# Row transposes as row pairs, and one layer norm on GpSimd, in a two-chain recurrent attention kernel

## The chip, the cores and the metric

The kernel runs on one core of a Trainium2 chip. Five engines work side by side in it: TensorE (PE; its weight loads are listed as PEld), VectorE (DVE), ScalarE (ACT), GpSimd (POOL) and SyncE (SP), which only issues transfers here. The metric is the device time of one execution in microseconds (us), the median of the runs. Lower is better.

## The reference, cut to what matters

Four layers in a row, each on the layer norm of its input and with a residual: attention with a recurrent memory (A), a gated feed-forward (B), A again and B again, with the same weights both times.

```
x = x + A(layernorm(x), mem0, Wq, Wk, Wv, Wo, seg_len=32)
x = x + B(layernorm(x), W_gate, W_up, W_down)
x = x + A(layernorm(x), mem0, Wq, Wk, Wv, Wo, seg_len=32)
x = x + B(layernorm(x), W_gate, W_up, W_down)

A: mem = mem0                                  # 8 rows of 448
   for each of 64 segments of 32 rows:
       h = concat(mem, rows)                   # 40 x 448
       p = softmax(mask(h Wq (h Wk)^T / 16))   # 16 heads of 256; rows are causal, memory is seen by all
       o = (p h Wv) Wo
       mem, out = o[:8], o[8:]
B: (relu(x W_gate) * (x W_up)) W_down          # 448 -> 1792 -> 448
```

x is 2048 x 448 in bf16. A segment needs the memory that the segment before it left, so attention is a chain of 64 links.

## The kernel before, in words

**Preparation.** Wq and Wk of each head are multiplied into one 448 x 448 matrix (tiles A_sb, A3, A3z), Wv and Wo into another (B_sb). Per head, scores are then rows x A x rows^T, and the output is p x rows x B. This ends some 72 us into the execution.

**Steps.** The rest is 69 steps (L591, `step(g, ff)`; the last, g = 68, only projects). The two attention layers run as two chains: step g does segment g of the first (chain 0) and segment g - 4 of the second (chain 1), in one set of matmuls; the chain is a block of columns (64 apart) of the transposed rows hT. From g = 4 to 63 both chains run, at the ends only one. Scores and weights for new memory rows (Sm, PM) and for segment rows (Sx, PX) are kept apart; hf is the half of the heads.

**Order.** TensorE's instructions keep the order in which the program writes them (`in_order`, L73). The tile framework sets the semaphores and picks the PSUM bank of each tile: seven banks serve all tiles of the tag "ps", the eighth the tag "ox". The order on VectorE and ScalarE follows the program but for small exchanges between neighbours.

Within a step of both chains TensorE does, in this order:

1. Queries: banks of PSUM named `prj`, six query tiles each. `open_banks` (L500) issues the part of the contraction over the last 64 of the 448 dimensions. It is done in *row pairs*: two matmuls of 64 rows each, one on partitions 0 to 63 and one on 64 to 127, in two banks. `close_bank` (L513) adds three full-height matmuls (128 rows) for each tile, 36 in all for two banks, 12 for the smaller banks z0 and z1, and has the bank copied to TQ (VectorE or ScalarE, 128x480) or TZ (64x320 on VectorE, then 64x320 on ScalarE). Order: open b0, b2; close b0, b2; open b1, b3, z0, z1; close z0, b1, b3; `hk_make`; close z1; open c0, c2, c1, c3; scores Sm(0); close c0, c2, c1, c3. b and z0 are heads' half 0, c and z1 half 1; z0's and z1's `prj` rows show as A3z and A_sb.
2. `hk_make` (L604): four full 128x128 transposes of hT into kps, copied to hk (rows in token order) by VectorE (128x512, L609) and, for the last 64 dimensions twice over, by ScalarE (L610).
3. PM is transposed (`flipped`: TensorE pps, VectorE copy PT), Sx(0) is made, and `weigh_m` multiplies hk by PT (ya, yb). In odd steps the feed's transposes tps follow. Then Sm(1) and Sx(1).
4. `project_out` (tile ox, B_sb as weights), the second half's weights, `project_tail`, `finish` (L726), which writes the new memory columns of hT (VectorE) and the attention output OT (ScalarE).

**The feed.** Odd steps from 3 on carry a feed-forward block (`Feed`, L400) among these: rows 0 to 63 of its tiles belong to the second B layer, 64 to 127 to the first. `residual` (L411) transposes OT back to rows (four full transposes, otp), adds them to xa (VectorE, L415, 128x448) and has `row_stats` (L156) take mean and variance (VectorE) and 1 / sqrt (GpSimd, L163 and L164). It stands between the closing of b2 and the opening of b1. `norm` (L418) calls `normed` (L167): two VectorE instructions, 448 and 64 columns, that write xn. It stands behind the closing of c0. `xposed` (L421) transposes xn (tps) into xT for the gate and up matmuls (`gate_up`, row pairs again: gate on one half of the rows, up on the other). `norm2` (L454) is the norm of the rows that go to the second attention chain; it too calls `normed`. A last feed runs by itself behind all steps.

**Row pairs elsewhere.** `flipped_rows` (L573) already transposes PM and PX in row pairs (ppr): for each 64-row half a transpose with a bank of its own, between matmuls of `gate_up`.

Of the kernel before, what the change touches and what calls it, by code (L numbers as in the profile page):

```python
# [8 lines left out]
BF = mybir.dt.bfloat16  # L9
F32 = mybir.dt.float32  # L10
I32 = mybir.dt.int32
AF = mybir.ActivationFunctionType
ALU = mybir.AluOpType
AX = mybir.AxisListType

DM = 448
# [15 lines left out]
HI = 128  # L32
HW = 5 * HI
W = 2 * L
# [6 lines left out]
ROWS = (slice(0, 64), slice(64, 128))  # L41
# [12 lines left out]
def build_kernel(ctx, tc, A_x, A_mem0, A_Wq, A_Wk, A_Wv, A_Wo, B_W_gate, B_W_up, B_W_down, out,  # L54
                 ntiles=16, nseg=64):
    nc = tc.nc
    P = nc.NUM_PARTITIONS
# [10 lines left out]
    psum = ctx.enter_context(tc.tile_pool(name="psum", bufs=7, space=bass.MemoryType.PSUM))  # L68
# [4 lines left out]
    def in_order(r):  # L73
        if last_pe[0] is not None:
            tc.add_manual_dep(r.ins, last_pe[0],
                              mybir.DependencyInfo(mybir.DependencyClass.NoSync,
                                                   mybir.DependencyReason.DATA),
                              reason="order of issue")
        last_pe[0] = r.ins.name

    def mm(*a, **k):
        in_order(nc.tensor.matmul(*a, **k))  # L82

    def tr(*a):
        in_order(nc.tensor.transpose(*a))  # L85

    def evac(eng, dst, src):
        if eng is nc.scalar:
            nc.scalar.copy(dst, src)  # L89
        else:  # L90
            eng.tensor_copy(dst, src)  # L91
# [8 lines left out]
    ident = glob.tile([P, P], BF, name="ident")  # L100
# [19 lines left out]
    for b in range(4):  # L120
        o = 0 if b % 2 == 0 else MEM
# [17 lines left out]
    for i in range(2):  # L139
        t = glob.tile([P, BLK, HW], BF, name=f"hT{i}")  # L140
# [10 lines left out]
    for hf in range(2):  # L151
        t = glob.tile([P, 5, 6, 64], BF, name=f"TQ{hf}")
        tc.keep_in_program_order(nc.gpsimd.memset(t[:], 0.0))
        TQ.append(t)

    def row_stats(t, pin=False):  # L156

        stats = p_ln.tile([P, nc.vector.BN_STATS_DIM], F32, tag="ln_stats")
        (tc.keep_in_program_order if pin else lambda i: i)(nc.vector.bn_stats(stats[:], t[:]))
        mv = p_ln.tile([P, 2], F32, tag="ln_mv")  # L160
        nc.vector.bn_aggr(mv[:], stats[:])
        rstd = p_ln.tile([P, 1], F32, tag="ln_rstd")
        nc.gpsimd.tensor_scalar(out=rstd[:], in0=mv[:, 1:2], scalar1=EPS, scalar2=None, op0=ALU.add)  # L163
        nc.gpsimd.tensor_tensor(out=rstd[:], in0=rstd[:], in1=half[:], op=ALU.pow)  # L164
        return t, mv, rstd

    def normed(stat):  # L167

        t, mv, rstd = stat
        xn = p_ln.tile([P, 512], BF, tag="ln_xn", bufs=3)  # L170
        for a, b, o in ((0, DM, 0), (384, DM, DM)):
            tc.keep_in_program_order(
                nc.vector.tensor_scalar(out=xn[:, o:o + b - a], in0=t[:, a:b], scalar1=mv[:, 0:1],  # L173
                                        scalar2=rstd[:], op0=ALU.subtract, op1=ALU.mult))
        return xn

# [201 lines left out]
    for hf in range(2):  # L378
        for name, shape, where in (("Y", [P, NT, W], YY[hf]), ("Z", [P, NT, W], YY[hf]), ("TZ", [P, 5, 128], TZ),
                                   ("PX", [P, 4, 64], PX), ("PM", [P, 2, 64], PM)):  # L380
            t = main.tile(shape, BF, name=f"{name}{hf}")
# [6 lines left out]
    OT = main.tile([P, 4, 128], BF, name="OT")  # L388
# [5 lines left out]
    for i in range(2):  # L394
        t = main.tile([P, 6, 128], BF, name=f"hk{i}")
# [4 lines left out]
    class Feed:  # L400
# [8 lines left out]
            self.nx = xp[i % 2]  # L409

        def residual(self):  # L411
            tp = psum.tile([P, 4, 128], BF, tag="ps", name="otp")
            for kd in range(4):
                tr(tp[:, kd, :], OT[:, kd, :], ident[:])
            nc.vector.tensor_tensor(self.x[:], tp[:].rearrange("p k d -> p (k d)")[:, 0:DM], self.x[:], op=ALU.add)  # L415
            self.st = row_stats(self.x)

        def norm(self):  # L418
            self.xn = normed(self.st)

        def xposed(self):  # L421
            tps = transpose_tokens(self.xn)
# [50 lines left out]
    def moving(hb, j, idx, chains, rows=slice(0, P)):  # L473

        if len(chains) == 2:
            return hb[rows, j, idx * HI:(idx + 1) * HI].rearrange("p (c k) -> p c k", k=64)[:, :, 0:L]
        c = chains[0]
        return hb[rows, j, idx * HI + 64 * c:idx * HI + 64 * c + L]
# [14 lines left out]
    def last_rows(hf, t):  # L493

        if t >= 24:
            return hf, A3z[ROWS[hf], t - 24, :]
        kd, eo, p4 = t // 8, t // 4 % 2, t % 4
        return eo, A3[ROWS[eo], hf, 4 * kd + p4, :]

    def open_banks(chains, hb, j, *which):  # L500

        n = L * len(chains)
        banks = [Bank(hf, i) for hf, i in which]
        for a, b in zip(banks[::2], banks[1::2]):
            for k in range(len(a.tiles)):
                for bk in (a, b):
                    t = bk.tiles[k]
                    r, w = last_rows(bk.hf, t)
                    mm(bk.out(t, n), w, moving(hb, j, 3, chains, ROWS[r]), start=(k == 0), stop=False,
                       skip_group_check=True)  # L510
        return banks

    def close_bank(bk, chains, hb, j, eng):  # L513

        n = L * len(chains)
        hf, N = bk.hf, len(bk.tiles)
        for t in bk.tiles:
            for kd in range(3):
                mm(bk.out(t, n), A_sb[:, kd, hf, t, :], moving(hb, j, kd, chains), start=False, stop=(kd == 2),
                   skip_group_check=True)  # L520
        ps = bk.ps
        if bk.i < 4:
            at = 2 * (bk.i // 2) + bk.i % 2
            parts = [(eng, slice(0, P), TQ[hf][:].rearrange("p g (k b) w -> p g k (b w)", b=2)[:, :, :, 32 * at:32 * at + 32], 3)]
        else:
            parts = [(nc.vector, slice(0, 64), TZ[hf][0:64, :, 0:64].unsqueeze(2), 1),
                     (nc.scalar, slice(64, 128), TZ[hf][0:64, :, 64:128].unsqueeze(2), 1)]
        for eng, rows, T, K in parts:
            T = T.rearrange("p g k (t q) -> p k t g q", q=16)
            if len(chains) == 2:  # L530
                evac(eng, T, ps[rows, 0:N * n].rearrange("p (k t g q) -> p k t g q", k=K, t=N // K, q=16))
                continue
            c = chains[0]
            src = ps[rows, 0:N * n].rearrange("p (k t w) -> p k t w", k=K, t=N // K)
            x, m = (0, SEG) if c == 0 else (MEM, 0)
            evac(eng, T[:, :, :, 2, MEM * c:MEM * c + MEM], src[:, :, :, m:m + MEM])
            evac(eng, T[:, :, :, 3 * c:3 * c + 2, :],
                 src[:, :, :, x:x + SEG].rearrange("p k t (g q) -> p k t g q", q=16))
# [47 lines left out]
    def active(g):  # L586
        return [c for c in (0, 1) if 0 <= g - c * LAG < nseg]
# [3 lines left out]
    def step(g, ff):  # L591
        chains = active(g)
        xs = active(g - 1)
        ms = [c for c in chains if g - c * LAG + 1 < nseg]
        gb, j = divmod(g, BLK)
        hb = hTb[gb % 2]
        cols = [(0, 32) if c == 0 else (48, 80) for c in xs] + [(32, 40) if c == 0 else (40, 48) for c in ms]
        lo, hi = min(a for a, _ in cols), max(b for _, b in cols)
        ox = psum.tile([P, 3, W], F32, tag="ox", bufs=1, name="ox")

        def ys(hf, later=0):
            return YY[hf][(g + later) % 2]

        def hk_make():  # L604
            kps = psum.tile([P, 4, 128], BF, tag="ps", name="kps")
            for i in range(4):
                tr(kps[:, i, :], hb[:, j, i * HI:(i + 1) * HI], ident[:])
            hk = HK[g % 2]
            nc.vector.tensor_copy(hk[:, 0:4, :], kps[:])  # L609
            nc.scalar.copy(hk[:].rearrange("p k n -> p (k n)")[:, 512:768].rearrange("p (a b) -> p a b", b=64)[:, 0::3, :],  # L610
                           kps[:, 3, :].rearrange("p (a b) -> p a b", b=64))
            return hk

        def scores_m(hf):
# [80 lines left out]

        def project_out(hf, t0, t1):

            for t in range(t0, t1):
                for mc in range(3):
                    mm(ox[:, mc, lo:hi], B_sb[:, hf, t, mc * 128:(mc + 1) * 128],  # L700
                       ys(hf)[:, t, lo:hi], start=(hf == 0 and t == 0 and mc == 0),
                       stop=(hf == 1 and t == NT - 1 and mc == 2), skip_group_check=True)
# [53 lines left out]
        close_bank(b2, chains, hb, j, nc.scalar)  # L756
        if ff is not None:
            ff.residual()
        b1, b3, z0, z1 = open_banks(chains, hb, j, (0, 1), (0, 3), (0, 4), (1, 4))
        close_bank(z0, chains, hb, j, None)  # L760
        load_some()
        close_bank(b1, chains, hb, j, nc.vector)
        close_bank(b3, chains, hb, j, nc.scalar)
        hk = hk_make()
        close_bank(z1, chains, hb, j, None)
        c0, c2, c1, c3 = open_banks(chains, hb, j, (1, 0), (1, 2), (1, 1), (1, 3))
        scores_m(0)
        close_bank(c0, chains, hb, j, nc.scalar)
        if ff is not None:
            ff.norm()  # L770
        close_bank(c2, chains, hb, j, nc.scalar)
        close_bank(c1, chains, hb, j, nc.vector)
        close_bank(c3, chains, hb, j, nc.scalar)
# [63 lines left out]
    for g in range(nsteps + 1):  # L837
        if g == LAG - 1:
            set_mem(LAG, mem0T[:].unsqueeze(2), (1,))
        i = (g - 3) // 2  # L840
        step(g, Feed(i) if g % 2 and 0 <= i < nblk + LAG // BLK - 1 else None)

    ff = Feed(nblk + LAG // BLK - 1)
# [65 lines left out]
```

## Time and profile before

| what | value |
|---|---|
| median of 3 runs | 1597.05 us (1596.65 to 1598.61) |
| the profiled execution | 1598.77 us |
| its span, first to last instruction | 1597.0 us |
| mean granted TensorE clock | 0.991 |
| an even and an odd step together, at 687 us | 44.95 us |

The profile describes one execution, which took 1598.77 us in all. A row of the timeline has the start (us from the span's start), the time to the end of the last instruction merged into the row, engine, line, operation, the tile written and the tiles read, partitions x elements, and the count; a bracket at its end says how long the engine idled before it and whom it waited for. A row of groups has the count, then the busy time in us and the mean of one in ns, then the idle time before them. Starts on TensorE are measured, ends are modelled, so the distance between two starts says what an instruction cost there.

### The profile page before, as it was taken

Reading aid. Unit: us, or ns where it says so; the run is one execution under the profiler, and the core shown is the slowest. Engines: PE = TensorE matmul, PEld = TensorE weight load, DVE = VectorE, ACT = ScalarE, POOL = GpSimd, SP = SyncE. Lnnn points to the kernel's source line nnn. Section 1 sums busy time; section 2 is a strip of 40 time slices with the busy share of each in tenths; the row PEclk is TensorE's granted clock in tenths of the full one; section 3 lists DMA queues with packets and bytes.
Section 4 is the critical chain, followed back from the end, with each engine's and each line's share of the span. In section 5 each row is a group of like instructions: output and inputs, shape, how many; then the busy total and the mean of one; then the engine's idle time right before and its main releaser. Section 6 shows DMA issues by size and latency. Waiting matters only on the chain.

```text
span 1597.0 us, 97098 instructions
## 1 busy us (share of the span) xinstructions
PE 1563.3 (98%) x44708; PEld 1433.4 (90%) x44708; DVE 1139.9 (71%) x3857; ACT 762.1 (48%) x2239; POOL 93.3 (6%) x242
## 2 busy tenths in 40 slices
PE   8989999999999999999999999999999999999997
PEld 6578899999999999999999999999999999999886
DVE  6756677777777777777777777777777777777773
ACT  6634444544444444544444445544444445544442
POOL 3110000000000000000000000000000000000000
PEclk9979999999999999999999999999999999999999
DMA  9530000000000000000000000000000000000000
GB/s 288 135 85 8 9 9 5 9 9 10 10 10 10 10 9 5 9 9 10 10 10 10 10 10 4 10 9 10 10 10 9 10 10 4 10 8 7 7 7 6
DMA packets 29464, 33.06 MB, mean 21 GB/s; under 512 B 3320, under 2 KB 28160, under 8 KB 29056
## 3 DMA queue, kind: packets, MB, share of 16 engines
q1 hardware_dynamic: 28992, 26.85, 6.3%
q8 instruction: 349, 5.72, 1.5%
q14 instruction: 59, 0.48, 0.1%
q0 software_dynamic: 64, 0.01, 0.0%
HBM read 23.18 MB, written 1.84 MB: 16 GB/s over the span
## 4 chain that ended last, share of the span: by engine, by line
PE 89%; DVE 7%; ACT 1%; issue 1%; DMA 1%; POOL 1%; SPq 0%; ACTq 0%; POOLq 0%; DVEq 0%
PE prj L82 25%; PE ox L82 25%; PE ups L82 10%; PE dps L82 6%; PE o L82 5%; PE y L82 4%; PE Sx L82 2%; PE Sm L82 2%; PE bps L82 1%; DVE TQ L91 1%; DVE xn L173 1%; PE aps L82 1%; PE tps L85 1%; PE pps L85 1%; PE kps L85 1%
## 5 line engine op out<-in xcount | busy, mean ns | idle before, releaser
L82 PEld LDWEIGHTS <-B_sb 128*128 128x128 bf16 (+1 forms) x15456 | 495.0, 103 | 29.2 <-issue 21.3
L82 PE MATMUL prj<-hT,A_sb 128*128 128x80 bf16 (+1 forms) x11424 | 441.6, 200 | 0.0
L82 PEld LDWEIGHTS <-A_sb 128*128 128x128 bf16 x11424 | 412.1, 100 | 8.3
L82 PE MATMUL ox<-Y,B_sb 128*128 128x80 bf16 (+4 forms) x5880 | 222.9, 198 | 1.8 <-DVE Y L643 1.8
L82 PE MATMUL ox<-Z,B_sb 128*128 128x80 bf16 (+2 forms) x5712 | 217.6, 199 | 1.3 <-DVE Z L643 1.3
L89 ACT CAST TQ<-prj 128x480 bf16<-128x480 f32 (+1 forms) x380 | 178.5, 497 | 83.6 <-PE prj L82 59.3
L82 PE MATMUL ups<-xT,Wgu_sb 64*128 64x128 bf16 (+1 forms) x3332 | 191.5, 214 | 2.2 <-issue 1.0
L82 PE MATMUL gps<-xT,Wgu_sb 64*128 64x128 bf16 (+1 forms) x3332 | 191.5, 214 | 0.3 <-ACT xT L425 0.3
L82 PEld LDWEIGHTS <-Wgu_sb 64*128 64x128 bf16 x6664 | 179.7, 95 | 5.5 <-issue 3.3
L91 DVE CAST TQ<-prj 128x480 bf16<-128x480 f32 (+1 forms) x228 | 129.2, 573 | 13.5 <-PE prj L82 11.3
L439 DVE SCALAR_TENSOR_TENSOR hh<-gps,ut 128x256 bf16<-128x256 f32 (+1 forms) x238 | 95.3, 407 | 48.9 <-ACT ut L438 36.4
L438 ACT CAST ut<-ups 128x256 bf16<-128x256 f32 (+1 forms) x238 | 85.4, 359 | 84.3 <-PE gps L82 66.1
L91 DVE CAST Y<-y 64x128 bf16<-64x128 f32 (+2 forms) x256 | 102.0, 419 | 13.3 <-ACT Y L89 4.3
L89 ACT CAST Y<-y 64x128 bf16<-64x128 f32 (+2 forms) x256 | 89.3, 379 | 45.6 <-DVE Y L91 42.0
L91 DVE CAST Z<-y 64x128 bf16<-64x128 f32 (+2 forms) x256 | 99.1, 418 | 12.4 <-ACT Z L89 5.5
L570 DVE COPY PT<-pps 128x128 bf16<-128x128 bf16 (+1 forms) x206 | 49.5, 254 | 79.7 <-PE pps L85 78.2
L89 ACT COPY hT<-tps 128x256 bf16<-128x256 bf16 x32 | 11.9, 372 | 197.4 <-DVE hT L91 197.4
L552 ACT ACTIVATE se<-se 128x80 f32<-128x80 f32 (+1 forms) x270 | 71.4, 298 | 67.4 <-DVE se L551 66.6
L89 ACT CAST TZ<-prj 64x320 bf16<-64x320 f32 (+2 forms) x152 | 56.2, 380 | 98.9 <-DVE TZ L91 94.3
L89 ACT CAST Z<-y 64x128 bf16<-64x128 f32 (+2 forms) x256 | 89.2, 378 | 23.8 <-DVE Z L91 17.4
L82 PEld LDWEIGHTS <-hk 40*128 40x128 bf16 (+1 forms) x1989 | 80.0, 94 | 18.6 <-issue 8.7
L558 DVE TENSOR_REDUCE ssum<-se 128x2 f32<-128x80 f32 (+1 forms) x270 | 70.8, 274 | 36.0 <-ACT se L552 33.7
(128 smaller groups left out, 2240.0 us busy)
## 6 DMA issues: line engine op xcount, KB each, us to landing
wo<-in_A_Wo_dram SPq DMA_DIRECT2D x8, 448.0 KB, 8.6
nat<-in_A_Wq_dram SPq DMA_DIRECT2D x8, 384.0 KB, 5.9
nat<-in_A_Wk_dram SPq DMA_DIRECT2D x8, 384.0 KB, 5.9
nat<-in_A_Wv_dram SPq DMA_DIRECT2D x8, 384.0 KB, 7.4
xa<-in_A_x_dram SPq DMA_DIRECT2D x32, 56.0 KB, 2.8
xa<-xp SPq DMA_DIRECT2D x32, 56.0 KB, 1.9
out_dram<-xa SPq DMA_DIRECT2D x32, 56.0 KB, 2.7
xp<-in_A_x_dram SPq DMA_DIRECT2D x30, 56.0 KB, 2.1
```

The lines of the kernel that those rows point to most:

```text
L82: in_order(nc.tensor.matmul(*a, **k))
L85: in_order(nc.tensor.transpose(*a))
L89: nc.scalar.copy(dst, src)
L91: eng.tensor_copy(dst, src)
L173: nc.vector.tensor_scalar(out=xn[:, o:o + b - a], in0=t[:, a:b], scalar1=mv[:, 0:1], scalar2=rstd[:], op0=ALU.subtract, op1=ALU.mult))
L438: nc.scalar.copy(ut[:, :, n], ups[:, :, n])
L439: nc.vector.scalar_tensor_tensor(out=hh[:, 2 * u:2 * u + 2, n], in0=gps[:, :, n], scalar=0.0, in1=ut[:, :, n], op0=ALU.max, op1=ALU.mult)
L552: nc.scalar.activation(se[:], se[:], AF.Exp, scale=SCALE)
L558: nc.vector.tensor_reduce(ssum[:], se[:], axis=AX.X, op=ALU.add)
L570: nc.vector.tensor_copy(PT[:], pps[:].rearrange("p b q -> p (b q)"))
```

## The change

There are three parts.

- A helper `flipped_dims` makes the same transposes in row pairs: eight of 64 rows to 64 columns, alternating between the halves of the partitions, each half into a bank of its own, the first into the "ox" bank, the second into a "ps" bank. `residual` and `hk_make` use it. The residual add becomes two instructions, 64-column pieces of 0, 128, 256, 384 and of 64, 192, 320. The copy of hk is split: columns of the first row half on VectorE, of the second on ScalarE; ScalarE's copy of the last dimensions reads the second bank. ox itself is now allocated by the first `project_out` of a step.
- `hk_make` moves behind the closing of z1, directly ahead of the opening of c0, c2, c1 and c3. The copies that belong to z1 move ahead of hk's with it.
- Attention's norm in the feed, `ff.norm`, moves from behind c0 to directly behind the residual, and its two instructions go to GpSimd. `norm2` and the norm of the last feed stay on VectorE.

```diff
+    def flipped_dims(name, src):
+        two = [psum.tile([P, 4, 64], BF, name=name, **where) for where in (dict(tag="ox", bufs=1), dict(tag="ps"))]
+        for kd in range(4):
+            for r in range(2):
+                tr(two[r][:, kd, :], src(r, kd), ident[ROWS[r], ROWS[r]])
+        return two
...
-    def normed(stat):
+    def normed(stat, eng=None):
...
-                nc.vector.tensor_scalar(out=xn[:, o:o + b - a], in0=t[:, a:b], scalar1=mv[:, 0:1],
+                (eng or nc.vector).tensor_scalar(out=xn[:, o:o + b - a], in0=t[:, a:b], scalar1=mv[:, 0:1],
...
         def residual(self):
-            tp = psum.tile([P, 4, 128], BF, tag="ps", name="otp")
-            for kd in range(4):
-                tr(tp[:, kd, :], OT[:, kd, :], ident[:])
-            nc.vector.tensor_tensor(self.x[:], tp[:].rearrange("p k d -> p (k d)")[:, 0:DM], self.x[:], op=ALU.add)
+            tp = flipped_dims("otp", lambda r, kd: OT[ROWS[r], kd, :])
+            xd = self.x[:].rearrange("p (c d) -> p c d", d=64)
+            for r in range(2):
+                nc.vector.tensor_tensor(xd[:, r::2, :], tp[r][:, 0:4 - r, :], xd[:, r::2, :], op=ALU.add)
...
         def hk_make():
-            kps = psum.tile([P, 4, 128], BF, tag="ps", name="kps")
-            for i in range(4):
-                tr(kps[:, i, :], hb[:, j, i * HI:(i + 1) * HI], ident[:])
+            kps = flipped_dims("kps", lambda r, kd: hb[ROWS[r], j, kd * HI:kd * HI + HI])
             hk = HK[g % 2]
-            nc.vector.tensor_copy(hk[:, 0:4, :], kps[:])
+            for r, eng in enumerate((nc.vector, nc.scalar)):
+                evac(eng, hk[:, 0:4, 64 * r:64 * r + 64], kps[r][:])
             nc.scalar.copy(hk[:].rearrange("p k n -> p (k n)")[:, 512:768].rearrange("p (a b) -> p a b", b=64)[:, 0::3, :],
-                           kps[:, 3, :].rearrange("p (a b) -> p a b", b=64))
+                           kps[1][:, 3, :].unsqueeze(1).to_broadcast([P, 2, 64]))
...
         if ff is not None:
             ff.residual()
+            ff.norm(nc.gpsimd)
         b1, b3, z0, z1 = open_banks(chains, hb, j, (0, 1), (0, 3), (0, 4), (1, 4))
...
         close_bank(b3, chains, hb, j, nc.scalar)
+        close_bank(z1, chains, hb, j, None)
         hk = hk_make()
-        close_bank(z1, chains, hb, j, None)
         c0, c2, c1, c3 = open_banks(chains, hb, j, (1, 0), (1, 2), (1, 1), (1, 3))
         scores_m(0)
         close_bank(c0, chains, hb, j, nc.scalar)
-        if ff is not None:
-            ff.norm()
         close_bank(c2, chains, hb, j, nc.scalar)
```

More of the change, by code (lines that the diff above doesn't have):

```diff
@@ L411, in residual, with norm @@
         def residual(self):
-            tp = psum.tile([P, 4, 128], BF, tag="ps", name="otp")
-            for kd in range(4):
-                tr(tp[:, kd, :], OT[:, kd, :], ident[:])
-            nc.vector.tensor_tensor(self.x[:], tp[:].rearrange("p k d -> p (k d)")[:, 0:DM], self.x[:], op=ALU.add)
+            tp = flipped_dims("otp", lambda r, kd: OT[ROWS[r], kd, :])
+            xd = self.x[:].rearrange("p (c d) -> p c d", d=64)
+            for r in range(2):
+                nc.vector.tensor_tensor(xd[:, r::2, :], tp[r][:, 0:4 - r, :], xd[:, r::2, :], op=ALU.add)
             self.st = row_stats(self.x)
-        def norm(self):
-            self.xn = normed(self.st)
+        def norm(self, eng=None):
+            self.xn = normed(self.st, eng)
         def xposed(self):
@@ L598, in step @@
         lo, hi = min(a for a, _ in cols), max(b for _, b in cols)
-        ox = psum.tile([P, 3, W], F32, tag="ox", bufs=1, name="ox")
+        ox = None
         def ys(hf, later=0):
@@ L696, in project_out @@
         def project_out(hf, t0, t1):
+            nonlocal ox
+            if ox is None:
+                ox = psum.tile([P, 3, W], F32, tag="ox", bufs=1, name="ox")
             for t in range(t0, t1):
```

## The prediction

> **What bounds the kernel now.** I read the page first (shares of the engines, then the chain that ended last), then one steady period of two steps in the view by windows.
>
> ```profile
> PE 1563.3 (98%) x44708; PEld 1433.4 (90%) x44708; DVE 1139.9 (71%) x3857; ACT 762.1 (48%) x2239; POOL 93.3 (6%) x242
> ...
> PE 89%; DVE 7%; ACT 1%; issue 1%; DMA 1%; POOL 1%; SPq 0%; ACTq 0%; POOLq 0%; DVEq 0%
> ```
> ```profile
> 687.27:732.22 44.95, 44.85 (x1287) 41.84 (x1283) 32.94 (x112) 21.77 (x64) 2.10 (x6) 1.00 0.04 9
> ```
>
> TensorE is busy 44.85 us of the 44.95 us that an even and an odd step take together; the columns behind it are weight loads, VectorE 32.94, ScalarE 21.77, GpSimd 2.10, then the granted clock, 1.00. So the time is TensorE's issue order. But a matmul's row lasts some 0.2 us while the next one starts 0.03 us later, so a short stall does not show as idle time. I therefore read the starts in the timeline and look for steps that are too long.
>
> TensorE's timeline of an odd step, around the two groups of transposes that are changed (start, length of the merged run, count at the end):
>
> ```profile
> 706.94 0.39 PE L85 MATMUL otp<-ident,OT 128*128 128x128 bf16 x4
> 707.26 0.39 PE L82 MATMUL prj<-hT,A 64*128 64x80 bf16 x12
> ...
> 707.72 1.90 PE L82 MATMUL prj<-hT,A_sb 128*128 128x80 bf16 x48
> 709.45 0.39 PE L85 MATMUL kps<-ident,hT 128*128 128x128 bf16 x4
> 709.68 0.59 PE L82 MATMUL prj<-hT,A_sb 128*128 128x80 bf16 x12
> 710.20 0.60 PE L82 MATMUL prj<-hT,A 64*128 64x80 bf16 x24
> 710.74 0.28 PE L82 MATMUL Sm<-hT,TQ 128*128 128x80 bf16 x3
> ...
> 710.89 2.75 PE L82 MATMUL prj<-hT,A_sb 128*128 128x80 bf16 x72
> 713.47 0.22 PE L85 MATMUL pps<-ident,PM 128*128 128x128 bf16 x1
> ```
>
> Three prices come out of the starts. A full-height matmul of 80 columns: 48 from 707.72 to 709.45, 1.73 us, 0.036 each. A full transpose: 709.45 to 709.68, 0.23 us for four, 0.057 each. The turn from full-height work to work in row pairs: 709.68 to 710.20 is 0.52 for twelve matmuls that need 0.43, so the turn costs 0.09 more. The otp group, 706.94 to 707.26, is 0.32: four transposes and one such turn. Neither group is late; they cost what they issue.
>
> The third place is further down the step. TensorE, odd step, then the same place in the even step:
>
> ```profile
> 713.91 0.18 PE L82 MATMUL Sx<-hT,TZ 128*128 128x40 bf16 x1
> 714.18 0.27 PE L82 MATMUL ya<-PT,hk 128*128 128x128 bf16 x2
> ...
> 714.40 0.39 PE L85 MATMUL tps<-ident,xn 128*128 128x128 bf16 x4
> ```
> ```profile
> 695.64 0.18 PE L82 MATMUL Sx<-hT,TZ 128*128 128x40 bf16 x1
> 695.74 0.27 PE L82 MATMUL ya<-PT,hk 128*128 128x128 bf16 x2
> ```
>
> From the last Sx to the first ya are 0.27 us in the odd step and 0.10 in the even. ya waits for PT, and VectorE's rows say why (odd step, then even):
>
> ```profile
> 707.60 0.38 DVE L415 TENSOR_TENSOR xa<-otp,xa 128x448 bf16<-128x448 bf16 x1
> ...
> 711.09 0.24 DVE L549 TENSOR_REDUCE mx<-Sm 128x2 f32<-128x80 f32 x1 [0.30 <-PE Sm L82]
> ...
> 712.67 0.24 DVE L563 TENSOR_TENSOR PM<-se,rs 128x80 bf16<-128x80 f32 x1
> 712.83 0.60 DVE L173 TENSOR_SCALAR xn<-xa,mv,rstd 128x448 bf16<-128x448 bf16 x2
> 713.34 0.65 DVE L91 CAST TQ<-prj 128x480 bf16<-128x480 f32 x1
> 713.91 0.22 DVE L570 COPY PT<-pps 128x128 bf16<-128x128 bf16 x1
> ```
> ```profile
> 694.76 0.66 DVE L91 CAST TQ<-prj 128x480 bf16<-128x480 f32 x1 [0.17 <-PE prj L82]
> ```
>
> In the odd step the norm (xn) stands between PM and bank c1's copy (TQ), so TQ starts 713.47 - 713.34 = 0.13 us before pps is issued; in the even step VectorE idles 0.17 waiting for the bank. TQ ends at 713.99, and PT, whose transposes were over by 713.69, queues behind it.
>
> **The change part by part.** How often each happens:
>
> ```profile
> L85 PE MATMUL kps<-ident,hT 128*128 128x128 bf16 x272 | 26.6, 221 | 0.0
> ...
> L85 PE MATMUL otp<-ident,OT 128*128 128x128 bf16 x136 | 13.2, 220 | 0.3 <-ACT OT L731 0.3
> ```
>
> 272 / 4 = 68 steps transpose rows, 136 / 4 = 34 feeds transpose attention output. Both chains run in 60 steps (g = 4 to 63), 30 of them odd, with a feed. In the others TensorE itself waits often; I count them apart.
>
> *Row pairs.* Eight transposes of 64 rows to 64 columns take the place of four full ones. The trace has this very form, within the gate and up matmuls:
>
> ```profile
> 718.70 0.19 PE L85 MATMUL ppr<-ident,PM 64*128 64x64 bf16 x2
> 718.73 0.22 PE L85 MATMUL ppr<-ident,PX 64*128 64x64 bf16 x4
> 718.78 0.22 PE L82 MATMUL ups<-xT,Wgu_sb 64*128 64x128 bf16 x1
> ```
>
> Six issue in 0.08 us, 0.028 a pair, so four pairs take 0.11. kps: 0.23 before, 0.11 after. It moves behind bank z1's twelve full-height matmuls, directly ahead of the pairs of c0 to c3, so the turn that stood there (0.09) now stands ahead of kps, and no turn is added. otp: it already stands at a turn, which moves from behind it to ahead of it; 0.23 of transposes become 0.11. Saved: 0.115 less some rounding, 0.11 each. 60 x 0.11 = 6.6 us for kps, 30 x 0.11 = 3.3 for otp.
>
> *Banks.* One half of each goes to the ox bank, so the seven others see the same number of tiles. The new waits are short: otp's first half needs the last ox matmul and OT, which it waited for already; kps's first half needs the residual add of otp's, at 708 in the odd step; project_out's ox now needs hk's copy, some 4 us ahead of it. I cost them at nothing.
>
> *Evacuation.* The residual add becomes two, of 256 and 192 columns; hk's copy becomes 256 columns on VectorE and 256 on ScalarE, behind z1's TZ copies.
>
> ```profile
> L570 DVE COPY PT<-pps 128x256 bf16<-128x256 bf16 x103 | 29.6, 288 | 73.8 <-PE pps L85 73.8
> L609 DVE COPY hk<-kps 128x512 bf16<-128x512 bf16 x68 | 28.8, 423 | 10.3 <-PE kps L85 7.7
> ...
> L91 DVE COPY PT<-ppr 128x192 bf16<-128x192 bf16 x33 | 8.4, 256 | 1.2
> ...
> L89 ACT COPY hT<-tps 128x256 bf16<-128x256 bf16 x32 | 11.9, 372 | 197.4 <-DVE hT L91 197.4
> ```
>
> 256 more columns cost VectorE 135 ns, 0.53 per column, so hk takes it 0.29 instead of 0.42. The add (0.38 for 448) has about 0.14 of fixed cost; a second one adds that, less the overlap of neighbours (TQ starts at 713.34, xn's run ends at 713.43: 0.09): 0.05, and I take 0.07. From the other side, if the stride of 64-column pieces halves its rate, 448 x 0.53 = 0.24 more, 0.31. I stay with 0.07: PT<-ppr writes 192 columns in strided pieces of 64 in 0.256, and 0.15 + 192 x 0.53 is 0.25, the full rate. A gain is excluded, since no column goes away. ScalarE:
>
> ```profile
> 709.77 0.56 ACT L89 CAST TQ<-prj 128x480 bf16<-128x480 f32 x1
> ...
> 710.88 0.42 ACT L89 CAST TZ<-prj 64x320 bf16<-64x320 f32 x1 [0.28 <-DVE TZ L91]
> 711.70 0.27 ACT L552 ACTIVATE se<-se 128x80 f32<-128x80 f32 x1 [0.40 <-DVE se L551]
> ...
> 713.73 0.56 ACT L89 CAST TQ<-prj 128x480 bf16<-128x480 f32 x1 [0.71 <-PE pps L85]
> ```
>
> It gets 0.37 more between b3's TQ and the exponential, where it idles 0.28 + 0.40 = 0.68. The exponential comes 0.22 earlier (TensorE gained that by then) and TQ 0.07 later: 0.68 - 0.37 - 0.29 leaves 0.02. If it runs over, PM is late; PM ends at 712.91 and pps comes at 713.47, so there is half a microsecond of cover. VectorE's 0.30 of idle time before mx covers its side: 0.30 - 0.22 - 0.07 + 0.13 = 0.14 left. Sm(0) needs b3's TQ, which would end at 709.77 + 0.56 + 0.07 = 710.40; Sm would issue at 710.74 - 0.22 = 710.52. Free by 0.12.
>
> *The norm on GpSimd.* It leaves VectorE after PM, so c1's copy starts when the bank is ready, PT follows pps as in the even step, and the 0.27 becomes 0.10: 30 x 0.17 = 5.1 us. What is late next is the even step's own 0.10, and Sm(1) behind tps, which needs c3's copy: that ends at 714.29 and Sm(1) comes 0.23 behind tps, at 714.63, so pulling it 0.17 nearer leaves room. The norm itself is hidden if it ends before tps.
>
> ```profile
> 709.26 0.57 POOL L164 TENSOR_TENSOR rstd<-rstd,half 128x1 f32<-128x1 f32 x1
> ```
> ```profile
> L382 POOL MEMSET Y<- 128x2240 bf16 x2 | 3.9, 1964 | 39.5 <-PE bps L82 39.4
> ```
>
> It starts at 709.83 + 0.07 = 709.9; tps would come at 714.40 - 0.39 = 714.01: 4.1 us. No row shows this operation on GpSimd. Lower bound: memset's 0.88 ns a column, 512 columns, 0.45 us. Upper bound: the one-column power's 0.57 us, were it all per column, would be far beyond the window. I take about 1 us, near the memset, the only row with many columns; GpSimd has nothing else until the next step's first copy.
>
> *The eight steps with one chain.* They wait in many places. At most they give 8 x 0.11 + 3 x 0.11 and the waits of tps for xn, 3.7 less the 2.8 of the tail feed, which keeps VectorE: 2.1 us. I take nothing and keep it for the low end.
>
> ```profile
> PE tps L85 <- DVE xn L173: 3.7, 4, 2.8
> ```
>
> Sum: 6.6 + 3.3 + 5.1 = 15.0 us. The profiled execution took 1598.77, which becomes 1583.8; it stands 1.7 above the median of the runs, 1597.05, so the median becomes **1582.0**.
>
> **Rivals.** *A: the odd step gives its 0.22 back at Sm(0).* If the split adds run at half rate, TZ, then ScalarE's copy of b3, come 0.31 later: 710.64, and 0.05 to be seen (PT ends at 714.13, ya starts at 714.18), against 710.52: 0.17 x 30 = 5.1 lost, 1587.1. For it: VectorE is packed from 707.60 on. Against: the rates above.
>
> *B: ya stays late.* ScalarE's spare time is only 0.02, and PT could meet another copy. Then 5.1 is missing, 1587.1. Against: the even step has the same order without the norm.
>
> *C: the change does not do what it says: the halves do not run side by side.* Each of eight transposes then costs 0.028, 0.22 for the group, no saving; 5.1 remain, 1592.0. Against: ppr's six in 0.08. The Trainium skill (TensorEngine Tiling, Instruction Overhead) speaks for it: about 60 cycles for each matmul, however few columns; at 2.4 GHz (TensorE: Matmul & The Clock Gate) an estimate of 25 ns, or 0.20 for eight. By that rule kps and otp would save 0.03 each and the time would be near 1589; the ppr rows, 0.014 per transpose, are against it.
>
> *D, slower: the norm on GpSimd ends after tps is due.* TensorE takes its work in order, so all behind tps waits, in 33 feeds. It decides from 4.1 us for the 512 columns, 8 ns each; at 4.55 us (0.45 x 33) the gain is gone; at 10 ns a column, 5.1 us, it costs 33 x 1.0 = 33, so 1582 + 33 = 1615. For it: the power row, 0.57 for a single column. Against: memset's 0.88 ns. The Trainium skill adds a way (SBUF — State Buffer, Who interferes with whom): a GpSimd instruction that reads SBUF and a VectorE instruction with two SBUF inputs shut each other out whole. Here that would be VectorE's rs and PM rows from 712.48 on, so by that rule nothing is lost unless the norm runs past 712.5; no row of before shows such a meeting.
>
> **How the numbers follow.** Forecast 0.68, A 0.12, B 0.08, C 0.06, D 0.05, and 0.01 that all of it cancels to no change. The forecast's own spread: 10 ns of reading in each of 120 places, about 1 us, and 2.1 below for the one-chain steps: 1579 to 1583. With A and B the range is 1578.5 to 1588, which holds 0.88 by these chances; C and D stay out. A measurement tells about 0.2%, 3.2 us, from no change. Faster by more: forecast, A, B, C, 0.94; within: 0.01; slower: 0.05.
>
> **What would show it.** Right: kps and otp as runs of eight that take 0.11 us to the next row; ya 0.10 after Sx in odd steps; a two-step period of 44.95 - 0.50 = 44.45 us; xn on GpSimd over before 712. Wrong: Sm(0) more than 0.15 after the pairs' end (A); 0.27 still ahead of ya (B); kps still 0.22 long (C); tps waiting for GpSimd (D). The forecast would be wrong altogether if the period's other stretches, which I took as fixed, shift when VectorE and ScalarE meet each other at new times.

## The result, and the profile after

| what | before | after |
|---|---|---|
| median of the runs made side by side | 1597.83 us (1596.65 to 1599.77, 4 runs) | 1581.26 us (1579.01 to 1582.62, 4 runs) |
| ratio | | 0.9893, 95% interval 0.9878 to 0.9907 |
| the profiled execution | 1598.77 us | 1579.01 us |
| its span | 1597.0 us | 1576.9 us |

The changed kernel is 16.6 us faster; the forecast was 1582.0. The engines' shares and the chain that ended last, from the page of the changed kernel:

```profile
PE 1547.3 (98%) x45116; PEld 1422.8 (90%) x45116; DVE 1112.7 (71%) x3825; ACT 783.3 (50%) x2307; POOL 174.9 (11%) x308
...
PE 94%; DVE 2%; ACT 1%; POOL 1%; issue 1%; DMA 0%; SPq 0%; POOLq 0%; ACTq 0%; DVEq 0%
```

TensorE is as full as before, with 408 matmuls more, and VectorE's share of the chain went from 7% to 2%. GpSimd works 82 us more and holds 1% of the chain, as before. The view by windows, one even and one odd step together:

```profile
676.64:721.11 44.47, 44.47 (x1299) 41.59 (x1295) 32.13 (x111) 22.38 (x66) 4.57 (x8) 1.00 0.04 9
```

The period fell from 44.95 to 44.47 us, and TensorE has no idle time in it at all. Where the 0.48 went is to be seen in TensorE's timeline of the odd step at the three places:

```profile
696.30 0.29 PE L85 MATMUL otp<-ident,OT 64*128 64x64 bf16 x8
696.43 0.38 PE L82 MATMUL prj<-hT,A 64*128 64x80 bf16 x12
...
699.14 0.29 PE L85 MATMUL kps<-ident,hT 64*128 64x64 bf16 x8
699.26 0.59 PE L82 MATMUL prj<-hT,A 64*128 64x80 bf16 x24
699.79 0.28 PE L82 MATMUL Sm<-hT,TQ 128*128 128x80 bf16 x3
...
702.52 0.22 PE L85 MATMUL pps<-ident,PM 128*128 128x128 bf16 x1
...
702.96 0.18 PE L82 MATMUL Sx<-hT,TZ 128*128 128x40 bf16 x1
703.06 0.27 PE L82 MATMUL ya<-PT,hk 128*128 128x128 bf16 x2
703.28 0.39 PE L85 MATMUL tps<-ident,xn 128*128 128x128 bf16 x4
```

Both groups of eight give way to the next row after 0.13 us (0.126 and 0.127 by the exact starts). kps is followed by the 24 pairs of c0 to c3 with no turn between: 699.26 to 699.79 is 0.53 for 24, the plain price. ya comes 0.10 behind the last Sx, where it took 0.27. By TensorE's starts, from a step's first query matmul to that of the next step, an even step went from 18.06 to 17.95 and an odd one from 26.89 to 26.51.

### The profile page after: what moved, and what is told of

Its sections match the earlier page's. It is cut to its first block, busy times and chain, and to the rows that moved or that the text cites. A ratio compares the mean times of both kernels' runs of the same rounds, so it can differ in the third digit from the quotient of the medians.

```text
span 1576.9 us, 98176 instructions
## 1 busy us (share of the span) xinstructions
PE 1547.3 (98%) x45116; PEld 1422.8 (90%) x45116; DVE 1112.7 (71%) x3825; ACT 783.3 (50%) x2307; POOL 174.9 (11%) x308
## 4 chain that ended last, share of the span: by engine, by line
PE 94%; DVE 2%; ACT 1%; POOL 1%; issue 1%; DMA 0%; SPq 0%; POOLq 0%; ACTq 0%; DVEq 0%
PE prj L82 29%; PE ox L82 25%; PE ups L82 10%; PE dps L82 6%; PE o L82 5%; PE y L82 4%; PE Sx L82 3%; PE Sm L82 2%; PE bps L82 1%; PE pps L85 1%; PE gps L82 1%; PE aps L82 1%; PE tps L85 1%; PE kps L85 1%; PE ym L82 1%
## 5 line engine op out<-in xcount | busy, mean ns | idle before, releaser
L82 PE MATMUL prj<-hT,A_sb 128*128 128x80 bf16 (+1 forms) x11424 | 430.6, 200 | 0.0
L82 PEld LDWEIGHTS <-A_sb 128*128 128x128 bf16 x11424 | 406.3, 100 | 8.3
L89 ACT CAST TQ<-prj 128x480 bf16<-128x480 f32 (+1 forms) x380 | 183.1, 494 | 82.8 <-PE prj L82 58.6
L171 POOL TENSOR_SCALAR rstd<-mv 128x1 f32<-128x1 f32 x67 | 15.2, 227 | 729.2 <-DVE mv L169 729.2
L82 PE MATMUL dps<-Wd_sb,hh 128*128 128x448 bf16 x476 | 96.0, 353 | 0.0
```

## The experiments

The theory was that of the prediction: three savings on TensorE's issue order that add up (rows 0.11 in each of 60 steps, attention output 0.11 and ya 0.17 in each of 30), while banks, copies and the norm on GpSimd are hidden. Against it stood that one of the three carries the gain alone, that the new place of the row transposes is the gain, that GpSimd rather than the place matters, or that the spare times which hide the rest are wider or narrower than read. Each run's ratio is taken to the kernel before, on the same chip. Where a run is set against the changed kernel, its median is compared with 1581.26 us, which was measured beside other runs of the kernel before; those gave 1597.83 there and 1597.38 to 1598.54 beside the experiments, so such a distance is good to some 1 to 2 us.

**Only the rows in pairs** (e1_rows_pairs), with `hk_make` as in the change and at its new place:

```diff
+        close_bank(z1, chains, hb, j, None)
         hk = hk_make()                      # in pairs
-        close_bank(z1, chains, hb, j, None)
```

> The kernel before with one part of the change: rows in row pairs behind z1, with the two banks and the split copy of hk; residual and norm as before. Theory (TensorE's issue order sets the time): in the changed kernel the run kps of eight takes 0.126 us, before the four took 0.225, so 60 steps x 0.10 = 6.0 us less, and up to 0.8 from the eight one-chain steps: 6 to 7 us under before. ya stays 0.27 behind Sx in odd steps. Rival (the parts need each other: VectorE sets the odd steps, and with the norm still on it they give back what TensorE gains): about 3 us less, only the even steps.

Measured: 1590.54 us against 1598.10, ratio 0.9952 (0.9934 to 0.9971): 7.6 us less. Norm and output are untouched, and TensorE's timeline in the odd step still shows ya 0.27 behind Sx:

```profile
707.37 0.18 PE L82 MATMUL Sx<-hT,TZ 128*128 128x40 bf16 x1
707.64 0.27 PE L82 MATMUL ya<-PT,hk 128*128 128x128 bf16 x2
```

So the pairs pay by themselves, a little more than the 6 to 7 us expected but within the interval, and do nothing for ya.

**Only the attention output in pairs** (e2_out_pairs):

```diff
-            tp = psum.tile([P, 4, 128], BF, tag="ps", name="otp")
+            tp = flipped_dims("otp", lambda r, kd: OT[ROWS[r], kd, :])
```

> The kernel before with one part: attention output in row pairs, two banks, two residual adds; rows and norm as before. Theory: the turn only moves, 0.225 us of transposes become 0.127, 33 x 0.10 = 3 us under before. Rival (the second add makes bank b3's copy late and Sm(0) waits for it): no gain, within 1 us of before, with Sm(0) more than 0.14 behind the last pair of the queries' opening.

Measured: 1595.23 against 1598.10, ratio 0.998 (0.997 to 0.999): 2.9 us less, near the 3.3 of the forecast. Sm(0) starts 0.54 us behind the first of the 24 pairs, as in the kernel before (710.20 to 710.74), so the second add delays nothing there.

**Only the norm on GpSimd, behind the residual** (e3_norm_gpsimd):

```diff
             ff.residual()
+            ff.norm(nc.gpsimd)
...
-            ff.norm()
         close_bank(c2, chains, hb, j, nc.scalar)
```

> The kernel before with one part: the feed's norm on GpSimd behind the residual; all transposes as before. Theory: ya comes 0.10 instead of 0.27 us behind Sx in odd steps, 30 x 0.17 = 5.1 us, and 0.9 more in the one-chain steps that waited for the norm: 5 to 6 us under before; even steps unchanged. Rival (ya was late because ScalarE or TensorE's own order makes PT late): ya stays at 0.2 or more, under 2 us gained.

Measured: 1593.44 against 1598.10, ratio 0.9964 (0.9951 to 0.9978): 4.7 us less, just under the 5 to 6 expected. TensorE's timeline of the odd step shows where:

```profile
714.05 0.18 PE L82 MATMUL Sx<-hT,TZ 128*128 128x40 bf16 x1
714.15 0.27 PE L82 MATMUL ya<-PT,hk 128*128 128x128 bf16 x2
```

The three parts alone give 7.6 + 2.9 + 4.7 = 15.2 us, all three together 16.6, within the intervals. The starts say it more closely: an odd step took 26.79, 26.79 and 26.72 us in the three runs against 26.89 before, so 0.10, 0.10 and 0.17 less, 0.37 together, and 0.38 less in the changed kernel; only the rows in pairs shorten the even step, to the same 17.95. The parts add up, and none stands on another.

**Only the new place, with full transposes** (e6_move_alone):

```diff
+        close_bank(z1, chains, hb, j, None)
         hk = hk_make()                      # four full transposes
-        close_bank(z1, chains, hb, j, None)
```

> The kernel before with the full transposes of rows moved behind z1 and nothing else. Theory: four full transposes cost 0.225 us in either place and no turn is added or removed, so the time is that of before within 1.5 us. Rival (the gain comes from where the transposes stand, because hk and TZ are copied in another order): 5 us or more under before.

Measured: 1599.19 against 1598.10, ratio 1.0005 (0.9994 to 1.0017): no difference. TensorE's timeline:

```profile
707.72 0.39 PE L85 MATMUL kps<-ident,hT 128*128 128x128 bf16 x4
708.04 0.60 PE L82 MATMUL prj<-hT,A 64*128 64x80 bf16 x24
```

0.32 for four full transposes and the turn, exactly what the otp group took in the kernel before: the turn stands behind kps now instead of behind z1's matmuls, and it costs the same.

**The pairs at the old place** (e5_pairs_old_place), the changed kernel with `hk_make` ahead of z1 again:

```diff
+        hk = hk_make()                      # in pairs
         close_bank(z1, chains, hb, j, None)
-        hk = hk_make()
```

> The changed kernel with the row pairs of kps back ahead of z1's full-height matmuls. Theory (a turn between full-height work and row pairs costs 0.09 to 0.10 us): two turns are added in each of 68 steps, 0.20 us a step, 12 to 13 us over the changed kernel, 3 to 5 under before. Rival (the saving is the pairing alone, the place is nothing): the time of the changed kernel.

Measured: 1594.16 against 1597.38, ratio 0.9974 (0.9964 to 0.9983); 12.9 us over the changed kernel. TensorE's timeline:

```profile
703.18 0.29 PE L85 MATMUL kps<-ident,hT 64*128 64x64 bf16 x8
703.40 0.60 PE L82 MATMUL prj<-hT,A_sb 128*128 128x80 bf16 x12
703.94 0.60 PE L82 MATMUL prj<-hT,A 64*128 64x80 bf16 x24
```

The eight take 0.22 to the next row instead of 0.13: a turn out of pairs lies behind them (0.09), and the turn into pairs ahead of c0 to c3 is there again (0.54 for twelve matmuls that need 0.43). Two turns more in each step cost more than the pairs save: an even step takes 18.16 us, 0.21 more than in the changed kernel and 0.10 more than in the kernel before. 12.8 of the 12.9 us lie in the 60 steps of both chains (1344.8 against 1332.0 by the starts). The place is worth nothing with full transposes; with pairs it decides between a gain and a loss.

**The norm on VectorE, in a gap** (e4_norm_vector_gap), the changed kernel with the norm's two instructions back on VectorE, between the exponential's input and the sum of the softmax of Sm(0):

```diff
-            ff.norm(nc.gpsimd)
...
-            weights_of(Sp, 2, PM[hf], blk[:], f"m{hf}")
+            begun = weights_begin(Sp, 2, PM[hf], blk[:], f"m{hf}")
+            if mid is not None:
+                mid()                       # ff.norm, on VectorE
+            weights_end(*begun)
```

> The changed kernel with the norm back on VectorE, but ahead of its old place: between the subtraction and the sum of Sm(0)'s softmax, where VectorE waits 0.39 us for ScalarE's exponential. Theory (what matters is that the norm no longer stands between PM and bank c1's copy, not which engine does it): PM is some 0.2 us later, which its 0.5 us of cover hides, ya stays 0.10 behind Sx, and the time is that of the changed kernel within 1.5 us, 15 to 18 under before. Rival (VectorE's load counts, GpSimd must take it): ya goes back towards 0.27 and about 5 us are lost, 11 to 12 under before.

Measured: 1581.94 against 1597.38, ratio 0.9903 (0.9887 to 0.992), the changed kernel's time. VectorE's timeline of the odd step:

```profile
701.80 0.24 DVE L559 TENSOR_TENSOR se<-Sm,mx 128x80 f32<-128x80 f32 x1
701.96 0.60 DVE L181 TENSOR_SCALAR xn<-xa,mv,rstd 128x448 bf16<-128x448 bf16 x2
702.47 0.23 DVE L566 TENSOR_REDUCE ssum<-se 128x2 f32<-128x80 f32 x1
...
703.46 0.66 DVE L91 CAST TQ<-prj 128x480 bf16<-128x480 f32 x1
```

xn fills the time in which VectorE waited for ScalarE's exponential, c1's copy is on time, and ya comes 0.10 behind Sx in all 60 steps. So the 5 us are not GpSimd's: they come from taking the norm out from between PM and c1's copy.

**Both halves in "ps" banks** (e8_both_ps):

```diff
-        two = [psum.tile([P, 4, 64], BF, name=name, **where) for where in (dict(tag="ox", bufs=1), dict(tag="ps"))]
+        two = [psum.tile([P, 4, 64], BF, name=name, **where) for where in (dict(tag="ps"), dict(tag="ps"))]
```

> The changed kernel with both halves of the transposes in banks of the seven, none in the ox bank. Theory (the ox bank is what makes the second bank free of cost): in odd steps the opening of z0 and z1 waits for bank b0's copy, 0.36 us, and Sm(0) for hk's copy, 0.18; in even steps Sm(0) for hk's copy, 0.19: 30 x 0.73 = 22 us over the changed kernel, so slower than before by about 5. Rival (a bank more or less is nothing, as I costed it): the time of the changed kernel.

Measured: 1602.66 against 1597.38, ratio 1.0034 (1.002 to 1.0049), 21.4 us over the changed kernel: slower than the kernel before. TensorE's timeline of the odd step:

```profile
710.96 0.20 PE L82 MATMUL prj<-hT,A3z 64*128 64x80 bf16 x1
711.32 0.30 PE L82 MATMUL prj<-hT,A3z 64*128 64x80 bf16 x7 [0.17 <-DVE TQ L91]
...
713.94 0.59 PE L82 MATMUL prj<-hT,A 64*128 64x80 bf16 x24
714.65 0.27 PE L82 MATMUL Sm<-hT,TQ 128*128 128x80 bf16 x3
```

The pair of z0 and z1 waits some 0.33 us until VectorE's copy frees a bank, and Sm(0) comes 0.71 behind the first of the 24 pairs instead of 0.53. By the starts, an odd step is 0.52 longer and an even one, which has only the second wait, 0.17: (0.52 + 0.17) x 30 = 20.7. The idle ox bank is what makes the split free.

**The norm made twice** (e7_norm_twice), the changed kernel with the two GpSimd instructions issued twice over the same tiles:

```diff
-        for a, b, o in ((0, DM, 0), (384, DM, DM)):
+        for a, b, o in ((0, DM, 0), (384, DM, DM)) * times:     # 2 for the norm on GpSimd
```

> The changed kernel with GpSimd doing the norm's two instructions twice over, the second time with the same values. It tests the slower rival's price. Theory: the two take 2.46 us from 699.27 in the changed kernel's trace; twice is 4.92, to 704.2, and tps is due at 703.28: it waits 0.95 us in each of 33 feeds, 31 us over the changed kernel, some 14 over before. VectorE's PM (two SBUF inputs) keeps its 0.24 us. Rival (a GpSimd instruction that reads SBUF shuts such a VectorE instruction out): PM or rs starts only when the 448-column instruction ends, near 703.6, pps and all behind it wait, and the time is 35 us or more over the changed kernel.

Measured: 1613.39 against 1597.38, ratio 1.0099 (1.0084 to 1.0114), 32.1 over the changed kernel. GpSimd's, then TensorE's, then VectorE's timeline of an odd step:

```profile
712.86 4.94 POOL L181 TENSOR_SCALAR xn<-xa,mv,rstd 128x448 bf16<-128x448 bf16 x4
```
```profile
716.76 0.28 PE L82 MATMUL yb<-PT,hk 128*128 128x128 bf16 x3
717.30 0.34 PE L85 MATMUL tps<-ident,xn 128*128 128x128 bf16 x3 [0.26 <-POOL xn L181]
717.86 0.23 PE L85 MATMUL tps<-ident,xn 128*128 128x128 bf16 x1 [0.22 <-POOL xn L181]
```
```profile
715.31 0.28 DVE L571 TENSOR_TENSOR PM<-se,rs 128x80 bf16<-128x80 f32 x1
```

GpSimd ends at 717.80, and tps, due 0.11 behind yb at 716.87, starts at 717.30 for the first three blocks and at 717.86 for the fourth. That is the slower rival's mechanism, reached by doubling. The sum came out, its division did not: by the starts an odd step is 0.83 us longer (27.34 against 26.51), not 0.95, and the 60 steps of both chains give 24.2 us; most of the rest lies in the three feeds beside one chain, where tps starts 2.1 to 2.2 us behind the last Sx instead of 0.03 to 0.05. In two odd steps, g = 5 and 49, PM took 0.65 and 0.57 us instead of 0.23; it had begun 0.18 and 0.25 us behind the start of a GpSimd instruction of 448 columns. (Both steps have two chains; the next expectation calls them one-chain steps.) The next two runs follow this up.

**The same doubling, grouped** (e9_norm_twice_grouped), so that rs of VectorE, which like PM reads two tiles of SBUF, begins while the second 448-column instruction has just started:

```diff
-        for a, b, o in ((0, DM, 0), (384, DM, DM)) * times:
+        for a, b, o in ((0, DM, 0),) * times + ((384, DM, DM),) * times:
```

> The changed kernel with the norm's GpSimd work doubled, as in the run with the norm made twice, but grouped: both 448-column instructions first, then both 64-column ones. The sum on GpSimd stays 4.94 us, so transposes of the norm come due and wait as in that run (1613.4). What moves is what meets the VectorE instructions with two SBUF inputs, rs<-rs,blk and PM<-se,rs: there the second 448-column instruction began 0.02 us before PM (which took 0.275 instead of 0.232), and in two one-chain steps PM began 0.18 and 0.25 us into one and took 0.65 and 0.57. Here rs begins 0.4 us into the second 448-column instruction in every odd step. If the two engines shut each other out for a whole instruction, rs ends only with it, some 1.3 us late, PM behind it, the transposes of PM wait about 0.9 us, and the kernel is 10 to 20 us slower than the doubled norm. If the loss is partial, as in those two rows, rs and PM take some 0.2 to 0.4 us more each, the half microsecond between PM and its transposes hides most of it, and the time stays within 4 us of the doubled norm. If those two rows had another cause, rs takes 0.16 and PM 0.23 to 0.24 as elsewhere, and the time is that of the doubled norm.

Measured: 1623.42 against 1598.54, ratio 1.0151 (1.0131 to 1.017). GpSimd's timeline (the whole run; then its second instruction by itself), and VectorE's:

```profile
716.36 5.11 POOL L181 TENSOR_SCALAR xn<-xa,mv,rstd 128x448 bf16<-128x448 bf16 x4
...
718.34 1.88 POOL L181 TENSOR_SCALAR xn<-xa,mv,rstd 128x448 bf16<-128x448 bf16 x1
```
```profile
718.41 0.17 DVE L568 RECIPROCAL rs<-ssum 128x2 f32<-128x2 f32 x1
718.61 0.46 DVE L570 TENSOR_TENSOR rs<-rs,blk 128x2 f32<-128x2 f32 x1
719.10 0.24 DVE L571 TENSOR_TENSOR PM<-se,rs 128x80 bf16<-128x80 f32 x1
```

rs takes 0.46 instead of 0.16, and PM behind it, still within the GpSimd instruction (718.34 to 720.22), its usual 0.24. In the 30 odd steps of both chains rs began 0.27 to 0.47 us behind the start of the GpSimd instruction; its end less its usual length lies at 0.57 us behind that start in every one of them, and the two PM of the run before come near it (0.58 and 0.60). So VectorE was held off for the first 0.57 us of a 1.88 us instruction, and not longer: partial, as in the second of the three expectations. The time missed that expectation, though: it was to stay within 4 us of the doubled norm and lies 0.5% higher, some 8 us by the two ratios. GpSimd's run itself became longer, 5.11 instead of 4.94 us, with gaps of 0.10 where an instruction writes again what the one ahead of it wrote; tps waits for it in 33 feeds, 33 x 0.17 = 5.6 us, and the odd step is longer by as much (27.51 against 27.34). The rest, 2 to 3 us, stays open.

**The two GpSimd instructions in the other order** (e10_tail_first):

```diff
-        for a, b, o in ((0, DM, 0), (384, DM, DM)):
+        for a, b, o in ((0, DM, 0), (384, DM, DM))[::-1 if eng is not None else 1]:
```

> The changed kernel with the two GpSimd instructions of the norm in the other order: 64 columns first, then 448. The 448 columns then end about 0.6 us later, at the time at which the pair ended before, 1.5 us before the transposes that read them. rs<-rs,blk of VectorE now begins 0.2 us before the end of the 448-column instruction. All theories expect the time of the changed kernel, 1579 to 1583. Whole exclusion: rs takes about 0.36 instead of 0.16 in odd steps and PM comes 0.2 later, inside its cover of half a microsecond. Partial: something between. No exclusion: rs 0.16, PM at its old place.

Measured: 1583.88 against 1598.54, ratio 0.9908 (0.9887 to 0.993), that of the changed kernel within the intervals, if 0.9 above the range expected. GpSimd's and VectorE's timelines:

```profile
699.60 2.46 POOL L181 TENSOR_SCALAR xn<-xa,mv,rstd 128x64 bf16<-128x64 bf16 x2
```
```profile
701.86 0.16 DVE L570 TENSOR_TENSOR rs<-rs,blk 128x2 f32<-128x2 f32 x1
702.05 0.24 DVE L571 TENSOR_TENSOR PM<-se,rs 128x80 bf16<-128x80 f32 x1
```

rs begins 1.7 us into the 448-column instruction and is not held off, which agrees with 0.57 and not with a whole instruction.

## Why the prediction was right

*What bounds the kernel.* Right: a period of 44.45 was forecast and 44.47 came, all of it TensorE.

*Row pairs.* The price of a group of eight was put at 0.11 and is 0.126: the first pair, behind the turn, takes 0.040, the other three 0.029 each, as in the six ppr rows. The saving per step held all the same (18.06 to 17.95 in the even step, 0.11), since the 24 pairs that stood behind the turn before take 0.53 now instead of 0.54; and alone the two edits gave 7.6 and 2.9 us where 6.6 and 3.3 were counted. That the turn only moves is shown by the run with full transposes at the new place (no difference) and by the run with pairs at the old one (12.9 us more).

*Banks at nothing.* Right, with the reason given: the first half goes where no "ps" tile waits. Without that the change would have been a loss of 5 us. The prediction had no rival for it, since the diff fixes the bank; the run shows how much hung on this line.

*Evacuation.* The split residual add was taken as 0.07 more. One row of the kernel before, which the prediction did not show, and then VectorE's timeline of the changed kernel:

```profile
708.02 0.63 DVE L159 BATCH_NORM_STATS2 stats<-xa 128x6 f32<-128x448 bf16 x1
```
```profile
696.87 0.45 DVE L423 TENSOR_TENSOR xa<-otp,xa 128x256 bf16<-128x256 bf16 x2
697.35 0.63 DVE L167 BATCH_NORM_STATS2 stats<-xa 128x6 f32<-128x448 bf16 x1
...
701.53 0.16 DVE L570 TENSOR_TENSOR rs<-rs,blk 128x2 f32<-128x2 f32 x1
701.72 0.24 DVE L571 TENSOR_TENSOR PM<-se,rs 128x80 bf16<-128x80 f32 x1
702.08 0.66 DVE L91 CAST TQ<-prj 128x480 bf16<-128x480 f32 x1
702.78 0.23 DVE L578 COPY PT<-pps 128x128 bf16<-128x128 bf16 x1
```

From the add to the statistics: 708.02 - 707.60 = 0.42 before, 697.35 - 696.87 = 0.48 now, 0.06 more. ScalarE's timeline:

```profile
699.09 0.56 ACT L89 CAST TQ<-prj 128x480 bf16<-128x480 f32 x1
699.54 0.38 ACT L89 COPY hk<-kps 128x256 bf16<-128x256 bf16 x1
699.95 0.42 ACT L89 CAST TZ<-prj 64x320 bf16<-64x320 f32 x1
700.39 0.27 ACT L617 COPY hk<-kps 128x128 bf16<-128x128 bf16 x1
700.76 0.27 ACT L560 ACTIVATE se<-se 128x80 f32<-128x80 f32 x1
```

ScalarE's new copy of hk stands ahead of TZ, not behind it as the program writes it and as I had placed it, and takes 0.38, where 0.37 was worked out. The exponential is on time behind it. b3's TQ ends at 699.65 and Sm(0) starts at 699.79: free by 0.14, where 0.12 was worked out. Rival A (1587.1) did not come; its condition, a residual add at half rate, did not hold. Rival B (1587.1) did not come either: ya is 0.10 behind Sx in all 60 steps, with c1's copy starting at 702.08, 0.44 ahead of pps (702.52).

*Rival C, the halves do not run side by side.* It did not come: 0.126 for eight, and within a pair the second half starts 0.004 behind the first. The rule of the Trainium skill (TensorEngine Tiling, Instruction Overhead) that stood for it, an estimate of 0.20 us for eight, does not agree with the trace here.

*The norm on GpSimd: a term that was mis-sized.* I took about 1 us, near the memset's 0.88 ns a column. GpSimd's timeline, then its groups with different shapes apart (count, then busy us and mean ns):

```profile
698.60 0.57 POOL L172 TENSOR_TENSOR rstd<-rstd,half 128x1 f32<-128x1 f32 x1
699.27 2.46 POOL L181 TENSOR_SCALAR xn<-xa,mv,rstd 128x448 bf16<-128x448 bf16 x2
```
```profile
L181 POOL TENSOR_SCALAR xn<-xa,mv,rstd 128x448 bf16<-128x448 bf16 x33 | 61.9, 1877 | 3.6
```

It is 2.46 us: 1.88 for 448 columns, 4.2 ns each, the rest for 64. It ends at 701.73, tps starts at 703.28, so 1.55 us are to spare, and the error did not reach the time. It was the point on which rival D (1615) hung, and the bound "decides from 4.1 us" was right: the doubled norm took 4.94 us, for which that rival's rule gives (4.94 - 4.1) x 33 = 28 us over the forecast, 1610, and the kernel took 1613.4; in the odd steps of both chains the rule's 0.84 came as 0.83. The step was right by the width of the window, not by the price. The line "xn over before 712", carried into this trace (2.2 us behind the end of the power, at 699.17), is missed by 0.4 us, with no harm.

*The eight steps with one chain.* Taken at 0 with 2.1 at most. The 60 steps of both chains gave 15.1 us by the starts (1347.1 to 1332.0), where the sum had 15.0. What the rest gave is not shown. In the two profiled executions the first four steps are 0.9 shorter and the end of the kernel 1.1, but these stretches differ by more than that between executions: in the run with the two GpSimd instructions in the other order, whose 60 steps took 1332.4, the first four were 1.3 shorter and the end 3.9 longer than in the changed kernel. Another 3.0 us between the two profiled executions lie in the preparation, which the change does not touch (the first query matmul starts at 71.9 and at 68.9 us). So the 15.0 us were right terms. That the forecast of 1582.0 met the measured time within 0.7 us is partly luck: the medians of the kernel before alone lie between 1597.05 and 1598.54.

*What stays open.* Of ya's 0.10 behind Sx, 0.025 is the plain distance; 0.075 is still a wait for PT. Its copy starts at 702.78, when c1's copy (702.08 + 0.66) and, by its modelled end, pps (702.52 + 0.22) are both just over, so which of the two holds it is not shown. No run tried to remove it.

## What to carry to other kernels

Where one engine's issue order is the time, count turns between full-height and row-pair work as instructions of their own (0.09 to 0.10 us here): pairs pay when they are put beside pairs and cost when they stand alone. A copy that must follow a transpose at once is delayed by whatever its engine does just ahead of it, so look for a gap on that engine before moving work to another one, which here gave the same time. When a moved operation has no row in the trace, put its place before its price: the width of the window decides, and a window four times the guess forgives a wrong guess.

## What the runs showed of the hardware that was not expected

- GpSimd held off a VectorE instruction that reads two tiles of SBUF, but only for the first 0.57 us of its 1.88 us instruction of 448 columns: rs took 0.46 us instead of 0.16 when it began 0.27 us behind it, and 0.16 when it began 1.7 us behind it. The RECIPROCAL, which reads one tile of SBUF, kept its 0.17 though it began 0.07 us behind it. The Trainium skill (SBUF — State Buffer, Who interferes with whom) calls the ports that the two engines share an exclusive lock, and says for VectorE's two-port modes that whoever issues first has them for the whole instruction. That the later one waits agrees here; a wait for the whole instruction, as the prediction read it, does not. The changed kernel itself showed this: rs began at 701.53, within GpSimd's 64 columns, which ended at 701.73, and took its 0.16. When both began together, GpSimd was delayed too: PM that began 0.02 us behind a 448-column instruction took 0.28 instead of 0.23, and the GpSimd instruction 1.95 instead of 1.88.
- A `TENSOR_SCALAR` with two operations on GpSimd in bf16 took 1.88 us for 448 columns and 0.59 for 64: by these two 3.3 ns a column and 0.38 us of fixed cost, nearly four times the column price of a memset there (0.88 ns).
- The turn from full-height to row-pair work on TensorE costs 0.098 us (0.134 instead of 0.036 to the first transpose of a group) and the one back some 0.09.
